# Attention and a squared-ReLU MLP on one core: direct cast loads and PE transposes for the first two batches, v on the software queue, attention ahead of the MLP

## The chip, the cores and the metric

The kernel runs on one core of one Trainium2 chip. The metric is the device time of one execution in microseconds (us). Engines are named as in the profile: PE does matmuls, DVE is VectorE, ACT is ScalarE, POOL is GpSimd, SP is SyncE, which here only issues DMA transfers. "Lnnn" is a line of the kernel. "DMA share" is the mean share of time that the 16 DMA engines of the core spent on packets; it passes 1 when packets overlap. "Clock" is the clock that the throttle granted to PE, as a fraction of full speed.

## The reference

```python
B, H, S, Nb, D = 8, 8, 576, 16, 64          # q, k, v: [B, H, S, D] float32
k_all = concatenate([beacon_k, k], axis=2)   # 16 beacon tokens in front
v_all = concatenate([beacon_v, v], axis=2)
scores = q @ k_all.T / sqrt(D)               # causal mask, beacons always visible
a = softmax(scores)
x = (a @ v_all)  -> [B*S, H*D] = [4608, 512]
h = x @ w_in                                 # w_in  [512, 2048] float32
out = (maximum(h, 0) ** 2) @ w_out           # w_out [2048, 512] float32
```

Attention is done per batch in four pairs of heads. For a pair it is a chain of links: QK (q times k, on PE), the exponential (ACT), the causal mask (DVE), AV (the result times v, on PE), the division by the sum (DVE, which writes x). The MLP is done in nine chunks of 512 tokens; a batch has 576 tokens, so chunk 0 needs batch 0, chunk 1 needs batch 1, and in general chunk j needs batch j (chunk 8 the last batch, 7). Matmuls are in bf16, so q, k, v and both weights must be cast; q and k must also be transposed (the head dimension has to lie on the partitions), and so must x.

## The kernel before

A small list scheduler written in Python decides, at build time, the order of instructions on every engine. An engine then runs its list in order, so an instruction whose data is late stops everything behind it on that engine. A gate holds a pair of heads back until the list has placed so many chunks of MLP work. The path of q and k of each batch is: load by SP into a float32 staging buffer (eight of them), cast by a compute engine, transpose by DMA.

```python
def add_load(b, x, c, prio):                 # 128 tokens of all heads: runs of 64 floats
    ...
    nc.sync.dma_start(out=st[lo:rows], in_=t[b, :, t0:t0 + rows - lo, :].transpose([1, 0, 2]))
    ...
    engs = ("DVE", "ACT", "POOL") if b == 0 else ("POOL",)
    cast[b, x, c] = add(..., engs, ..., emit_cast, deps=deps, give=ld)

def add_trans(b, x, prio):
    ...
            nc.sync.dma_start(               # DMA transpose, on the SP queue
                out=dst[b % 2][:, lo:hi, :, :].rearrange("p c h t -> p (c h) t"),
                in_=srcb[b % 2][:, lo:hi, :].rearrange("p c d -> p (c d)"),
                transpose=True)
...
def gate(o):                                 # when pair p may enter PE's list
    if p < HP: return True
    jj, i = divmod(p - HP, HP)
    return o.progress >= mlp_chunk_us * (jj + (0.0, 0.2, 0.4, 0.6)[i])
...
def add_xt(b):                               # x of a batch: five DMA transposes on the SP queue
    ...
    nc.sync.dma_start(out=xT[:, :, at:at + n], in_=xn[b % 2][0:n, t, :], transpose=True)
```

The weights are cast by their own transfers on the software queue of POOL, once the last load of batch 0 is there. (Cuts are marked with three dots.)

The softmax here doesn't subtract the row's maximum and nothing guards it: scores larger than these inputs give would overflow.

## Time and profile before

The median of three runs was 431.69 us (429.19 to 433.43); with a fourth it was 432.28 us.

| stretch, us | PE busy, us | clock | what happens |
|---|---|---|---|
| 0 to 72 | 14.6 | 0.77 | attention of batch 0, then PE waits for x |
| 72 to 130 | 49.6 | 0.82 | MLP chunk 0, then attention of batch 1 |
| 130 to 300 | 155.7 | 0.94 | steady state, with holes |
| 300 to 429 | nearly all | 0.99 | chunks 6 to 8, pure PE |

The view counts time without a clock record as 1.00. The packed trace's first clock record lies at 35.7 us here, so the clocks shown for the first stretches are too high by an amount that the records don't give.

The page's view of 40 equal slices (10.7 us each), the kernel before; digits are tenths:

```profile
PE   0174003998679995899799979997999999999995
...
PEclk9998555999858998699999989998999999999999
DMA  9799999996979998999899877056002201400202
```

PE is empty in the slices from 43 to 64 us while the DMA engines are full. The busy times of three stretches, the kernel before (after the stretch: its length, then busy us and instructions of PE, PEld, DVE, ACT, POOL, then clock, DMA share, GB/s):

```profile
0.00:72.00 72.00, 14.61 (x169) 8.76 (x170) 12.97 (x38) 17.94 (x24) 18.86 (x35) 0.77 1.08 180
72.00:130.00 58.00, 49.61 (x389) 25.02 (x388) 16.94 (x32) 31.04 (x36) 16.77 (x26) 0.82 0.93 182
130.00:300.00 170.00, 155.68 (x1214) 81.15 (x1213) 54.98 (x96) 84.81 (x96) 43.67 (x68) 0.94 0.89 170
```

The two longest waits of PE, the kernel before (total us, times, longest us):

```profile
PE ps_98 L476 <- DMA xT<-xn_85: 34.7, 1, 34.7
PE ps_95 L344 <- DMA qT_77<-qb_71: 19.7, 2, 15.6
```

PE starts 15.6 us late, because q must be loaded, cast and transposed, and it stands still for 34.7 us ahead of the first MLP matmul, because x must be transposed by DMA. The timeline of the SP queue and of PE, the kernel before, shows the end of that wait (start us, us, what, number):

```profile
52.07 11.26 SPq L431 DMA_TRANSPOSE xT<-xn_85  x5
63.43 8.16 SPq L294 DMA_TRANSPOSE qT_78<-qb_72  x1
...
71.65 3.57 PE L476 MATMUL ps_98<-xT,w_in 128*128 128x512 bf16 x8 [34.74 <-DMA xT<-xn_85]
```

x of batch 0 was complete at 38.4 us, but its transposes stand in SP's list behind the loads of batch 1, are issued only at 52 us, and then take 20 us among the weights. Chunk 1 starts at 128.0 us. The packets, the kernel before:

```profile
DMA packets 185422, 58.10 MB, mean 135 GB/s; under 512 B 176688, under 2 KB 180784, under 8 KB 185392
```

### The profile page before, as it was taken

The numbers are of one execution on the slowest core, as the hardware profiler recorded it, in microseconds if no ns is written. First come the engines' busy times: TensorE is split into PE (matmuls) and PEld (weight loads), VectorE is DVE, ScalarE is ACT, GpSimd is POOL, SyncE is SP. The second block draws the span as 40 slices with busy tenths as digits, with TensorE's granted clock in tenths as the row PEclk, the third lists the DMA queues.
The fourth block names the chain that finished last, engine by engine and source line by source line (L and its number), as shares of the span: only waits on it lengthen the run. The fifth ranks groups of instructions, "written<-read, shape, count | busy, mean of one in ns | idle before, by whom it ended". The sixth has DMA issues, their size and how long they took to land.

```text
span 429.2 us, 6367 instructions
## 1 busy us (share of the span) xinstructions
PE 343.5 (80%) x2560; PEld 171.7 (40%) x2560; DVE 124.4 (29%) x230; ACT 191.1 (45%) x219; POOL 79.3 (18%) x128
## 2 busy tenths in 40 slices
PE   0174003998679995899799979997999999999995
PEld 0033001443444443444444438644454445444442
DVE  1135000311433512252135224512541463130310
ACT  4470000518574447254555455635644664341621
POOL 3034330360123450243222410020000000000000
PEclk9998555999858998699999989998999999999999
DMA  9799999996979998999899877056002201400202
GB/s 168 156 188 197 203 176 195 209 172 151 212 139 189 229 199 187 198 211 188 185 189 199 179 159 147 2 131 146 1 2 73 81 2 50 106 2 0 98 2 98
DMA packets 185422, 58.10 MB, mean 135 GB/s; under 512 B 176688, under 2 KB 180784, under 8 KB 185392
## 3 DMA queue, kind: packets, MB, share of 16 engines
q1 hardware_dynamic: 181168, 53.50, 63.5%
q0 software_dynamic: 4224, 4.19, 6.0%
q8 instruction: 20, 0.33, 0.3%
q14 instruction: 10, 0.08, 0.1%
HBM read 37.22 MB, written 9.44 MB: 109 GB/s over the span
## 4 chain that ended last, share of the span: by engine, by line
PE 62%; SPq 4%; DMA 2%; ACT 2%; DVE 1%; issue 1%; ACTq 0%
PE ps_95 L511 8%; PE ps_96 L476 8%; PE ps_97 L476 7%; PE ps_95 L476 7%; PE ps_97 L511 7%; PE ps_98 L476 6%; PE ps_98 L511 5%; PE ps_96 L511 4%; SPq L294 3%; PE ps_98 L391 3%; SPq L431 1%; DMA xT<-xn_85 1%; PE ps_95 L391 1%; ACT pt_81 L365 1%; PE ps_96 L344 1%; PE ps_96 L391 1%
## 5 line engine op out<-in xcount | busy, mean ns | idle before, releaser
L476 PEld LDWEIGHTS <-w_in 128*128 128x128 bf16 x640 | 63.1, 101 | 109.7 <-issue 55.6
L476 PE MATMUL ps_98<-xT,w_in 128*128 128x512 bf16 (+1 forms) x136 | 33.0, 390 | 34.7 <-DMA xT<-xn_85 34.7
L500 DVE TENSOR_TENSOR g_88<-g_88 128x1024 bf16<-128x1024 bf16 x40 | 28.0, 701 | 93.2 <-ACT g_88 L488 93.2
L476 PE MATMUL ps_96<-xT,w_in 128*128 128x512 bf16 (+1 forms) x176 | 41.2, 384 | 5.4 <-DMA xT<-xn_85 4.5
L511 PEld LDWEIGHTS <-g_88 128*128 128x128 bf16 x320 | 29.8, 98 | 36.4 <-issue 3.1
L476 PE MATMUL ps_97<-xT,w_in 128*128 128x512 bf16 (+1 forms) x168 | 37.1, 367 | 1.9 <-DMA xT<-xn_86 1.9
L511 PEld LDWEIGHTS <-g_89 128*128 128x128 bf16 x256 | 23.7, 98 | 29.0 <-issue 2.8
L476 PE MATMUL ps_95<-xT,w_in 128*128 128x512 bf16 (+1 forms) x160 | 34.6, 361 | 0.0
L500 DVE TENSOR_TENSOR g_89<-g_89 128x1024 bf16<-128x1024 bf16 x32 | 22.3, 697 | 35.9 <-ACT g_89 L488 35.9
L511 PE MATMUL ps_95<-w_out,g_89 128*128 128x512 bf16 x128 | 30.4, 380 | 0.0
L511 PE MATMUL ps_97<-w_out,g_88 128*128 128x512 bf16 x128 | 30.0, 380 | 0.0
L488 ACT ACTIVATE g_88<-ps_98 128x1024 bf16<-128x1024 f32 x8 | 8.2, 1024 | 48.4 <-PE ps_98 L476 48.4
L344 PEld LDWEIGHTS <-kT_79 64*128 64x128 bf16 x192 | 8.7, 106 | 37.8 <-issue 33.1
L511 PE MATMUL ps_96<-w_out,g_88 128*128 128x512 bf16 x96 | 22.7, 379 | 0.0
L511 PE MATMUL ps_98<-w_out,g_89 128*128 128x512 bf16 x96 | 22.7, 379 | 0.0
L344 PE MATMUL ps_95<-qT_77,kT_79 64*128 64x128 bf16 (+3 forms) x38 | 6.0, 371 | 20.6 <-DMA qT_77<-qb_71 19.7
L488 ACT ACTIVATE g_88<-ps_96 128x1024 bf16<-128x1024 f32 x10 | 10.2, 1024 | 15.1 <-PE ps_96 L476 15.1
L374 DVE TENSOR_TENSOR pt_81<-pt_81,tri 128x1024 bf16<-128x1024 bf16 x8 | 5.5, 690 | 38.3 <-ACT pt_81 L365 38.3
L391 PEld LDWEIGHTS <-pt_81 128*128 128x128 bf16 (+1 forms) x240 | 11.9, 120 | 11.3 <-DVE pt_81 L374 8.5
L511 PE MATMUL ps_98<-w_out,g_88 128*128 128x512 bf16 x64 | 15.1, 379 | 0.0
L344 PEld LDWEIGHTS <-kT_80 64*128 64x128 bf16 x192 | 7.6, 96 | 16.4 <-issue 14.2
L374 DVE TENSOR_TENSOR pt_84<-pt_84,tri 128x1024 bf16<-128x1024 bf16 x8 | 6.6, 819 | 26.0 <-ACT pt_84 L365 26.0
(169 smaller groups left out, 466.1 us busy)
## 6 DMA issues: line engine op xcount, KB each, us to landing
out_dram<-osb_90 SPq DMA_DIRECT2D x9, 512.0 KB, 3.3
out_dram<-osb_91 SPq DMA_DIRECT2D x8, 512.0 KB, 3.5
w_in<-in_moe_w_in_dram POOLq DMA_DIRECT2D x4, 512.0 KB, 11.7
w_out<-in_moe_w_out_dram POOLq DMA_DIRECT2D x4, 512.0 KB, 12.8
stg_67<-in_k_dram SPq DMA_DIRECT2D x6, 256.0 KB, 4.2
stg_68<-in_k_dram SPq DMA_DIRECT2D x5, 256.0 KB, 4.2
stg_65<-in_q_dram SPq DMA_DIRECT2D x4, 256.0 KB, 4.8
stg_66<-in_q_dram SPq DMA_DIRECT2D x4, 256.0 KB, 4.3
```

The source lines that it names most:

```text
L294: nc.sync.dma_start(out=dst[b % 2][:, lo:hi, :, :].rearrange("p c h t -> p (c h) t"), in_=srcb[b % 2][:, lo:hi, :].rearrange("p c d -> p ( ...
L344: nc.tensor.matmul(st[:, hj, at:at + 128 * (t1 - t0)], kT[b % 2][hp, c, pr, :], qT[b % 2][hp, t0:t1, pr, :], start=True, stop=True,)
L365: nc.scalar.activation(pt[take_pt.held[2]][:, :, off:off + width], st[:, :, 0:width], AF.Exp, bias=0.0, scale=scale)
L374: nc.vector.tensor_tensor(out=d, in0=d, in1=tri[:, None].to_broadcast([128, 2, 4, 128]), op=ALU.min)
L391: nc.tensor.matmul(a[:, hj, t * (D + 1):(t + 1) * (D + 1)], P[0:rr, hj, o:o + 128], vb[b % 2][0:rr, c, h, :], start=(c == 0), stop=(c == t),)
L431: nc.sync.dma_start(out=xT[:, :, at:at + n], in_=xn[b % 2][0:n, t, :], transpose=True)
L476: nc.tensor.matmul(h[:, u, lo - spans[0][0]:hi - spans[0][0]], w_in_sb[:, mc, ft * 128:(ft + 1) * 128], xT[:, mc, lo % RING:lo % RING + hi ...
L488: nc.scalar.activation(dst, h, AF.Relu, bias=0.0, scale=1.0)
L500: nc.vector.tensor_tensor(out=d, in0=d, in1=d, op=ALU.mult)
L511: nc.tensor.matmul(o[:, ts, :], G[:, fc, (2 * u + ts) * 128:(2 * u + ts + 1) * 128], w_out_sb[:, fc, :], start=(fc == 0), stop=(fc == NFT ...
```

## The change

Its intent is to get PE going early. In batches 0 and 1, q and k come straight from DRAM in bf16, through the casting software queue, one pair of heads at a time, in runs of 1.5 KB (each partition takes six neighbouring tokens); PE transposes them, and also x of these batches. v of batches 1 to 7 moves from the SP queue to the software queue. The gates put attention 0.4 chunk ahead of the MLP. Smaller parts: QK computes 576 queries instead of 640, two buffers instead of one may hold attention output, the table of the exponential is loaded at the start, casts of batch 0 avoid ACT. The weights also start earlier: they wait for the fourth load of v instead of the last load of batch 0, and the traces show w_in issued at 10.3 us instead of 30.5. The diff, cut to its core:

```diff
+    NPE = 2          # batches with direct loads and PE transposes of q, k
+    NXPE = 2         # batches whose x is transposed by PE
...
+        soft = x == "v" and b >= 1
+        queue = nc.gpsimd if soft else nc.sync
...
+    def add_strided(b, prio):
...
+                    nc.gpsimd.dma_start(out=dst[b % 2][:, h],
+                                        in_=t[b, h].rearrange("h (p s) d -> p h s d", s=NS))
...
+                            nc.tensor.transpose(pp[64 * hj:64 * hj + 64, half, at + u * NP:at + (u + 1) * NP],
+                                                t[b % 2][:, 2 * pr + hj, u, :], ident[0:NP, 0:NP])
...
-            return o.progress >= mlp_chunk_us * (jj + (0.0, 0.2, 0.4, 0.6)[i])
+            return o.progress >= mlp_chunk_us * (jj + (-0.4, -0.15, 0.1, 0.35)[i])
...
+    def add_xt_pe(b):
...
+                    nc.tensor.transpose(pp[:, 0, t_start(t):t_start(t) + n],
+                                        xn[b % 2][0:n, t, 128 * pr:128 * pr + 128], ident[0:n, 0:n])
...
-            w_ops["in", i] = add(f"win{i}", "POOL", 1.3, emit, prio=-100 + i, deps=[load0[-1]], dma=3.2)
+            w_ops["in", i] = add(f"win{i}", "POOL", 1.3, emit, prio=-100 + i, deps=[load0[3]], dma=3.2)
```

More of the change, by code (lines that the diff above doesn't have):

```diff
@@ L7 @@
 from concourse._compat import with_exitstack
+from concourse.masks import make_identity
 FP32 = mybir.dt.float32
@@ L19 @@
     __slots__ = ("name", "engs", "dur", "emit", "prio", "need", "users", "left", "ready",
-                 "take", "give", "gate", "held", "dma", "tag", "pe_time")
+                 "take", "give", "gate", "held", "dma", "pe_time", "behind", "followers")
     def __init__(self, name, engs, dur, emit, prio=0.0, deps=(), take=None, give=None,
-                 gate=None, dma=0.0, pe_time=0.0):
+                 gate=None, dma=0.0, pe_time=0.0, behind=()):
         self.name = name
@@ L36, in __init__ @@
         self.pe_time = pe_time
+        self.behind = list(behind)
+        self.followers = []
 class Order:
-    LAT = {"PE": 0.2, "ACT": 0.2, "DVE": 0.15, "POOL": 0.25, "SP": 0.1}
+    LAT = {"PE": 0.2, "ACT": 0.2, "DVE": 0.15, "POOL": 0.25, "SP": 0.1, "-": 0.0}
     def __init__(self, pools, limits):
@@ L58, in run @@
     def run(self):
-        engines = ["PE", "ACT", "DVE", "POOL", "SP"]
+        engines = ["PE", "ACT", "DVE", "POOL", "SP", "-"]
         for op in self.ops:
-            op.left = len(op.need)
+            op.left = len(op.need) + len(op.behind)
             for d in op.need:
                 d.users.append(op)
+            for d in op.behind:
+                d.followers.append(op)
         avail = {e: [] for e in engines}
@@ L102, in run @@
                     for op in avail[e]:
-                        if id(op) in started:
+                        if any(free[x] <= now + 1e-9 for x in op.engs[:op.engs.index(e)]):
                             continue
@@ L122, in run @@
                     started.add(id(op))
+                    for u in op.followers:
+                        u.left -= 1
+                        if u.left == 0:
+                            release(u)
                     for ee in op.engs:
@@ L130, in run @@
                     dur = op.dur[e] if isinstance(op.dur, dict) else op.dur
+                    if e == "SP":
+                        dur = max(dur, dma_free - now - 4.0)
                     end = now + dur
@@ L149, in run @@
         for op, e, _ in issued:
-            op.emit(e)
+            if e != "-":
+                op.emit(e)
         self.issued = issued
@@ L193 @@
     stg = [sb(f"stg{i}", [128, H, D], FP32) for i in range(NSTG)]
-    qb = [sb(f"qb{i}", [128, NT, H * D], BF16) for i in range(2)]
-    kb = [sb(f"kb{i}", [128, NT, H * D], BF16) for i in range(2)]
+    NP = 96
+    NS = S // NP
+    W = HP * NT * 128
+    WS = H * NS * D
+    qk_area = sb("qk_area", [128, 4 * WS], BF16)
+    qb = [qk_area[:, (2 * i) * W:(2 * i + 1) * W].rearrange("p (g c d) -> p g c d", g=HP, c=NT)
+          for i in range(2)]
+    kb = [qk_area[:, (2 * i + 1) * W:(2 * i + 2) * W].rearrange("p (g c d) -> p g c d", g=HP, c=NT)
+          for i in range(2)]
+    qs = [qk_area[0:NP, (2 * i) * WS:(2 * i + 1) * WS].rearrange("p (h s d) -> p h s d", h=H, s=NS)
+          for i in range(2)]
+    ks = [qk_area[0:NP, (2 * i + 1) * WS:(2 * i + 2) * WS].rearrange("p (h s d) -> p h s d", h=H, s=NS)
+          for i in range(2)]
+    bks = [sb(f"bks{i}", [Nb, H, D], BF16) for i in range(2)]
     vb = [sb(f"vb{i}", [128, NT, H, D + 1], BF16) for i in range(2)]
-    qT = [sb(f"qT{i}", [128, NT, HP, 128], BF16) for i in range(2)]
-    kT = [sb(f"kT{i}", [128, NT, HP, 128], BF16) for i in range(2)]
+    qT = [sb(f"qT{i}", [128, HP, NT * 128], BF16) for i in range(2)]
+    kT = [sb(f"kT{i}", [128, HP, NT * 128], BF16) for i in range(2)]
     pt = [sb(f"pt{i}", [128, 2, 2048], BF16) for i in range(NPT)]
     xn = [sb(f"xn{i}", [128, NT, H * D], BF16) for i in range(2)]
+    ident = sb("ident", [128, 128], BF16)
+    warm = sb("warm", [128, 8], FP32)
     xT = sb("xT", [128, NMC, RING], BF16)
@@ L209 @@
         pools={"ps": range(4), "stg": range(NSTG), "pt": range(NPT)},
-        limits={"strip": 2, "av": 1, "mlp": 2},
+        limits={"strip": 2, "av": 2, "mlp": 2, "tp": 1},
     )
     add = order.add
+    nc.vector.memset(warm, 0.0)
+    nc.scalar.activation(warm, warm, AF.Exp)
     for i in range(2):
-        nc.gpsimd.memset(qb[i][:, NT - 1, :], 0.0)
-        nc.gpsimd.memset(kb[i][:, NT - 1, :], 0.0)
-    for i in range(2):
-        nc.vector.memset(qb[i][:, 0, :], 0.0)
-    nc.gpsimd.memset(tri, BIG)
-    for i in range(4):
-        nc.gpsimd.affine_select(out=tri[:, i, :], in_=tri[:, i, :], compare_op=ALU.is_ge, fill=0.0,
-                                base=Nb if i == 0 else 0, pattern=[[1, 128]], channel_multiplier=-1)
+        nc.vector.memset(kT[i][:, :, Nb + S:NT * 128], 0.0)
+        nc.vector.memset(vb[i][:, :, :, D:D + 1], 1.0)
     for p in pt:
@@ L225, with emit_tri @@
             nc.vector.memset(p[:, :, lo:hi], 0.0)
-    for i in range(2):
-        nc.vector.memset(vb[i][:, :, :, D:D + 1], 1.0)
+    nc.vector.memset(tri, BIG)
+    def emit_tri(e):
+        for i in range(4):
+            nc.gpsimd.affine_select(out=tri[:, i, :], in_=tri[:, i, :], compare_op=ALU.is_ge, fill=0.0,
+                                    base=Nb if i == 0 else 0, pattern=[[1, 128]], channel_multiplier=-1)
+    ident_op = add("ident", "POOL", 0.6, lambda e: make_identity(nc, ident), prio=-199.8)
+    tri_op = add("tri", "POOL", 1.0, emit_tri, prio=-150.0)
     def rows_of(c):
@@ L246, with t_rows, t_start, add_zero @@
     load0 = []
-    def q_rows(c):
-        return 128 - Nb if c == 0 else rows_of(c)
+    load_chain = []
+    def t_rows(t):
+        return 128 - Nb if t == 0 else rows_of(t)
+    def t_start(t):
+        return max(0, 128 * t - Nb)
+    NPE = 2
+    NXPE = 2
+    zero_ops = {}
+    strided = {}
+    def add_zero(b):
+        def emit(e):
+            nc.gpsimd.memset(qb[b % 2][:, :, NT - 1, :], 0.0)
+            nc.gpsimd.memset(kb[b % 2][:, :, NT - 1, :], 0.0)
+        deps = trans[NPE - 1, "q"] + trans[NPE - 1, "k"] + trans[NPE - 2, "q"] + trans[NPE - 2, "k"]
+        zero_ops[b] = add(f"zero{b}", "POOL", 1.0, emit, prio=10.0 * b - 1, deps=deps)
     def add_load(b, x, c, prio):
-        rows = q_rows(c) if x == "q" else rows_of(c)
         t, beacon = src[x]
-        box = {}
+        lo = Nb if (c == 0 and beacon is not None) else 0
+        if x == "q":
+            t0, rows = 128 * c, min(128, S - 128 * c)
+        else:
+            t0, rows = t_start(c), rows_of(c)
         def emit_load(e):
             st = stg[ld.held[2]]
-            lo = 0
-            if c == 0 and beacon is not None:
-                lo = Nb
-                nc.sync.dma_start(out=st[0:Nb], in_=beacon[b].transpose([1, 0, 2]))
-            t0 = max(0, 128 * c - Nb)
-            nc.sync.dma_start(out=st[lo:rows], in_=t[b, :, t0:t0 + rows - lo, :].transpose([1, 0, 2]))
-        ld = add(f"ld{b}{x}{c}", "SP", 1.3 if (c == 0 and beacon is not None) else 0.65, emit_load,
-                 prio=prio, take=("stg", "stg"), dma=1.15 * rows / 128)
+            if lo:
+                queue.dma_start(out=st[0:Nb], in_=beacon[b].transpose([1, 0, 2]))
+            queue.dma_start(out=st[lo:rows], in_=t[b, :, t0:t0 + rows - lo, :].transpose([1, 0, 2]))
+        soft = x == "v" and b >= 1
+        queue = nc.gpsimd if soft else nc.sync
+        ld = add(f"ld{b}{x}{c}", "POOL" if soft else "SP", 1.3 if lo else 0.65, emit_load,
+                 prio=prio, take=("stg", "stg"), dma=1.15 * rows / 128,
+                 behind=[strided[0][1, "q"]] if b == 0 else load_chain[-1:] + [strided[min(b, NPE - 1)][HP - 1, "q"]], deps=[w_ops["out", 2]] if b == 1 else ())
+        load_chain.append(ld)
         if b == 0:
@@ L274, in emit_cast @@
             else:
-                dst = (qb if x == "q" else kb)[b % 2][0:rows, c, :]
-                copy_on(e, dst, st[0:rows].rearrange("p h d -> p (h d)"))
+                dst = (qb if x == "q" else kb)[b % 2][0:rows, :, c, :]
+                copy_on(e, dst, st[0:rows].rearrange("p (g u) d -> p g (u d)", u=2))
         deps = [ld]
-        if b >= 2:
-            if x == "v":
-                deps += [av_ops[p] for p in range(HP * (b - 2), HP * (b - 1))]
+        if x == "v" and b >= 2:
+            deps += [av_ops[p] for p in range(HP * (b - 2), HP * (b - 1))]
+        if x != "v":
+            if b < NPE + 2:
+                deps += [zero_ops[b]]
             else:
                 deps += trans[b - 2, x]
-        engs = ("DVE", "ACT", "POOL") if b == 0 else ("POOL",)
-        cast[b, x, c] = add(f"cast{b}{x}{c}", engs, {"DVE": 0.65, "ACT": 0.65, "POOL": 1.1}, emit_cast,
+        engs = ("POOL", "DVE") if b == 0 else ("POOL",)
+        cast[b, x, c] = add(f"cast{b}{x}{c}", engs, {"DVE": 0.6, "POOL": 0.65}, emit_cast,
                             prio=prio, deps=deps, give=ld)
@@ L289, in add_trans @@
         srcb, dst = (qb, qT) if x == "q" else (kb, kT)
-        groups = [(c, c + 1) for c in range(NT)] if b == 0 else [(0, NT)]
-        ops = []
-        for lo, hi in groups:
-            def emit(e, lo=lo, hi=hi):
-                nc.sync.dma_start(
-                    out=dst[b % 2][:, lo:hi, :, :].rearrange("p c h t -> p (c h) t"),
-                    in_=srcb[b % 2][:, lo:hi, :].rearrange("p c d -> p (c d)"),
-                    transpose=True,
-                )
-            deps = [cast[b, x, c] for c in range(lo, hi)]
-            if b >= 2:
-                deps += [qk_ops[p, i] for p in range(HP * (b - 2), HP * (b - 1)) for i in range(4)]
-            ops.append(add(f"tr{b}{x}{lo}", "SP", 0.4 + 0.64 * (hi - lo), emit, prio=prio, deps=deps,
-                           dma=0.64 * (hi - lo)))
@@ L304, in add_trans, with emit @@
-        trans[b, x] = ops
+        def emit(e):
+            nc.sync.dma_start(
+                out=dst[b % 2].rearrange("p g (c t) -> p (g c) t", c=NT),
+                in_=srcb[b % 2].rearrange("p g c d -> p (g c d)"),
+                transpose=True,
+            )
+        deps = [cast[b, x, c] for c in range(NT)]
+        deps += [qk_ops[p, i] for p in range(HP * (b - 2), HP * (b - 1)) for i in range(4)]
+        trans[b, x] = [add(f"tr{b}{x}", "SP", 3.8, emit, prio=prio, deps=deps, dma=3.2)]
@@ new lines, in add_strided, with emit_bk, emit, emit_tp @@
+    def add_strided(b, prio):
+        loads = {}
+        def emit_bk(e):
+            nc.gpsimd.dma_start(out=bks[b % 2], in_=beacon_k[b].transpose([1, 0, 2]))
+        after = [w_ops["out", 3]] if b == 1 else [strided[b - 1][HP - 1, "q"]] if b else []
+        free = trans[b - 2, "q"] + trans[b - 2, "k"] if b >= 2 else []
+        bk = None
+        trans[b, "q"], trans[b, "k"] = [], []
+        for pr in range(HP):
+            h = slice(2 * pr, 2 * pr + 2)
+            for n, (x, t, dst) in enumerate((("k", k, ks), ("q", q, qs))):
+                def emit(e, t=t, dst=dst, h=h):
+                    nc.gpsimd.dma_start(out=dst[b % 2][:, h],
+                                        in_=t[b, h].rearrange("h (p s) d -> p h s d", s=NS))
+                loads[pr, x] = add(f"sld{b}{x}{pr}", "POOL", 0.7, emit, prio=prio + pr + 0.1 * n, behind=after, deps=free,
+                                   dma=0.95)
+            if pr == 0:
+                bk = add(f"sldbk{b}", "POOL", 0.7, emit_bk, prio=prio + 0.05, behind=after, deps=free, dma=0.1)
+        strided[b] = loads
+        for pr in range(HP):
+            h = slice(2 * pr, 2 * pr + 2)
+            box = {}
+            def emit_tp(e, pr=pr, h=h, box=box):
+                pp = ps[box["t"].held[2]].bitcast(BF16)
+                nc.tensor.transpose(pp[:, 1, 0:Nb], bks[b % 2][:, h, :], ident[0:Nb, 0:Nb])
+                for half, at, t in ((1, Nb, ks), (0, 0, qs)):
+                    for u in range(NS):
+                        for hj in range(2):
+                            nc.tensor.transpose(pp[64 * hj:64 * hj + 64, half, at + u * NP:at + (u + 1) * NP],
+                                                t[b % 2][:, 2 * pr + hj, u, :], ident[0:NP, 0:NP])
+            busy = [qk_ops[HP * (b - 2) + pr, i] for i in range(4)] if b >= 2 else []
+            tp = add(f"tp{b}.{pr}", "PE", 1.3, emit_tp, prio=100.0 * (HP * b + pr) - 190,
+                     deps=[bk, loads[pr, "k"], loads[pr, "q"], ident_op] + busy, take=("ps", "tp"))
+            box["t"] = tp
+            def emit_k(e, pr=pr, box=box):
+                pp = ps[box["t"].held[2]].bitcast(BF16)
+                copy_on(e, kT[b % 2][:, pr, 0:Nb], pp[:, 1, 0:Nb])
+                copy_on(e, kT[b % 2][:, pr, Nb:Nb + S].rearrange("p (n s) -> p n s", s=NS),
+                        pp[:, 1, Nb:Nb + S].rearrange("p (s n) -> p n s", s=NS))
+            def emit_q(e, pr=pr, box=box):
+                pp = ps[box["t"].held[2]].bitcast(BF16)
+                copy_on(e, qT[b % 2][:, pr, 0:S].rearrange("p (n s) -> p n s", s=NS),
+                        pp[:, 0, 0:S].rearrange("p (s n) -> p n s", s=NS))
+            ek = add(f"ek{b}.{pr}", "DVE", 0.9, emit_k, prio=-200.0, deps=[tp])
+            eq = add(f"eq{b}.{pr}", ("DVE", "ACT"), 0.75, emit_q, prio=-199.0, deps=[tp])
+            add(f"tpg{b}.{pr}", "-", 0.0, None, prio=0.0, deps=[ek, eq], give=tp)
+            trans[b, "k"].append(ek)
+            trans[b, "q"].append(eq)
@@ L307 @@
     PIECES = [
-        ([(0, 0, 4, 0)], 0, 512),
-        ([(1, 1, 5, 0)], 512, 464),
-        ([(2, 2, 5, 0), (0, 4, 5, 336)], 1024, 416),
-        ([(3, 3, 5, 0), (4, 4, 5, 208)], 1536, 288),
+        ([(0, 0, 496, 0)], 0, 496),
+        ([(1, 112, 576, 0)], 512, 464),
+        ([(2, 240, 576, 0), (0, 496, 576, 336)], 1024, 416),
+        ([(3, 368, 576, 0), (4, 496, 576, 208)], 1536, 288),
     ]
@@ L315, in pt_off @@
         if c == 0:
-            return 128 * t if t < 4 else 1360
+            return t_start(t) if t < 4 else 1360
         if c == 4:
@@ L332, in gate @@
             jj, i = divmod(p - HP, HP)
-            return o.progress >= mlp_chunk_us * (jj + (0.0, 0.2, 0.4, 0.6)[i])
+            return o.progress >= mlp_chunk_us * (jj + (-0.4, -0.15, 0.1, 0.35)[i])
         exps = []
         for i, (mms, off, width) in enumerate(PIECES):
-            cols = sum(128 * (t1 - t0) for _, t0, t1, _ in mms)
+            cols = sum(max(96, t1 - t0) for _, t0, t1, _ in mms)
             def emit_qk(e, i=i, mms=mms):
@@ L344, in emit_qk @@
                         nc.tensor.matmul(
-                            st[:, hj, at:at + 128 * (t1 - t0)],
-                            kT[b % 2][hp, c, pr, :],
-                            qT[b % 2][hp, t0:t1, pr, :],
+                            st[:, hj, at:at + t1 - t0],
+                            kT[b % 2][hp, pr, 128 * c:128 * c + 128],
+                            qT[b % 2][hp, pr, t0:t1],
                             start=True, stop=True,
                         )
-            need_c = {c for c, _, _, _ in mms}
-            need_t = {t for _, t0, t1, _ in mms for t in range(t0, t1)}
-            if b == 0:
-                deps = [trans[b, "k"][c] for c in need_c] + [trans[b, "q"][t] for t in need_t]
+            if b < NPE:
+                deps = [trans[b, "k"][pr], trans[b, "q"][pr]]
             else:
@@ L357, in add_pair @@
             if i == 0:
-                take_pt = add(f"pt{p}", "POOL", 0.0, lambda e: None, prio=base, deps=deps,
+                take_pt = add(f"pt{p}", "-", 0.0, None, prio=base, deps=deps,
                               take=("pt", "pt"), gate=gate)
-            qk_ops[p, i] = add(f"qk{p}.{i}", "PE", 0.12 + cols / 2400.0, emit_qk, prio=base + i,
+            qk_ops[p, i] = add(f"qk{p}.{i}", "PE", 0.05 + cols / 2400.0, emit_qk, prio=base + i,
                                deps=deps + [take_pt], take=("ps", "strip"), gate=gate)
@@ L378, in emit_mask @@
                                     op=ALU.min)
-        mask = add(f"mask{p}", "DVE", 0.85, emit_mask, prio=base, deps=exps)
+        mask = add(f"mask{p}", "DVE", 0.95, emit_mask, prio=base, deps=exps + [tri_op])
         def emit_av(e):
@@ L422, with ring_deps, feeds @@
     s2_first = {}
+    def ring_deps(lo, hi):
+        deps = []
+        for j in range(NCH):
+            if j * TCH < hi - RING and (j + 1) * TCH > lo - RING:
+                deps += [s1_ops[j, f] for f in range(NFT // 2)]
+        return deps
+    def feeds(o, lo, hi):
+        for j in range(NCH):
+            if j * TCH < hi and (j + 1) * TCH > lo:
+                xt_of_chunk[j].append(o)
     def add_xt(b):
         for t in range(NT):
-            n = q_rows(t)
-            tok = b * S + max(0, 128 * t - Nb)
+            n = t_rows(t)
+            tok = b * S + t_start(t)
             def emit(e, n=n, t=t, tok=tok):
@@ L431, in emit, with emit_tp, emit_ev @@
                 nc.sync.dma_start(out=xT[:, :, at:at + n], in_=xn[b % 2][0:n, t, :], transpose=True)
-            deps = [norm_ops[HP * b + i] for i in range(HP)]
-            for j in range(NCH):
-                if j * TCH < tok + n - RING and (j + 1) * TCH > tok - RING:
-                    deps += [s1_ops[j, f] for f in range(NFT // 2)]
-            o = add(f"xt{b}.{t}", "SP", 1.2, emit, prio=-50.0 + b, deps=deps, dma=0.64 * n / 128)
-            xt_ops[b, t] = o
-            for j in range(NCH):
-                if j * TCH < tok + n and (j + 1) * TCH > tok:
-                    xt_of_chunk[j].append(o)
+            deps = [norm_ops[HP * b + i] for i in range(HP)] + ring_deps(tok, tok + n)
+            o = add(f"xt{b}.{t}", "SP", 1.28, emit, prio=-50.0 + b, deps=deps, dma=0.64 * n / 128)
+            xt_ops[b, t] = o
+            feeds(o, tok, tok + n)
+    def add_xt_pe(b):
+        for pr in range(HP):
+            box = {}
+            def emit_tp(e, pr=pr, box=box):
+                pp = ps[box["t"].held[2]].bitcast(BF16)
+                for t in range(NT):
+                    n = t_rows(t)
+                    nc.tensor.transpose(pp[:, 0, t_start(t):t_start(t) + n],
+                                        xn[b % 2][0:n, t, 128 * pr:128 * pr + 128], ident[0:n, 0:n])
+            tp = add(f"xtp{b}.{pr}", "PE", 0.35, emit_tp, prio=-120.0, deps=[norm_ops[HP * b + pr]],
+                     take=("ps", "tp"))
+            box["t"] = tp
+            def emit_ev(e, pr=pr, box=box):
+                pp = ps[box["t"].held[2]].bitcast(BF16)
+                copy_on(e, xT[:, pr, (b * S) % RING:(b * S) % RING + S], pp[:, 0, 0:S])
+            o = add(f"xte{b}.{pr}", ("ACT", "DVE"), {"ACT": 0.67, "DVE": 0.72}, emit_ev, prio=-110.0,
+                    deps=[tp], give=tp)
+            xt_ops[b, pr] = o
+            feeds(o, b * S, b * S + S)
     w_ops = {}
@@ L481, in add_chunk @@
             s1_ops[j, f] = add(f"s1.{j}.{f}", "PE", 1.73, emit_s1, prio=base + f,
-                               deps=xt_of_chunk[j] + [w_ops["in", f // 2]], take=("ps", "mlp"), pe_time=1.73)
+                               deps=xt_of_chunk[j] + [w_ops["in", f // 2]] + [s2_ops[j - 2, u] for u in range(2) if j >= 2], take=("ps", "mlp"), pe_time=1.73)
             def emit_relu(e, f=f):
@@ L500, in emit_sq @@
                 nc.vector.tensor_tensor(out=d, in0=d, in1=d, op=ALU.mult)
-            sq.append(add(f"sq{j}.{f}", "DVE", 0.62, emit_sq, prio=-10.0, deps=[rl]))
+            sq.append(add(f"sq{j}.{f}", "DVE", 0.7, emit_sq, prio=-10.0, deps=[rl]))
         for u in range(2):
@@ L547 @@
     st_ops = {}
-    b0 = [("k", 0), ("q", 0), ("q", 1), ("q", 2), ("q", 3), ("k", 1), ("q", 4), ("k", 2), ("k", 3), ("k", 4)]
+    nat = [("k", 0), ("q", 0), ("q", 1), ("q", 2), ("q", 3), ("k", 1), ("q", 4), ("k", 2), ("k", 3), ("k", 4)]
     for b in range(B):
-        n = 0
         lp = 10.0 * b
-        for x, c in b0 + [("v", c) for c in range(NT)]:
+        if b < NPE:
+            add_strided(b, lp - 200.0 if b == 0 else lp)
+        if NPE <= b < NPE + 2:
+            add_zero(b)
+        for n, (x, c) in enumerate(([] if b < NPE else nat) + [("v", c) for c in range(NT)]):
             add_load(b, x, c, lp + 0.1 * n)
-            n += 1
-        add_trans(b, "k", lp - 5.0)
-        add_trans(b, "q", lp - 5.1)
+        if b >= NPE:
+            add_trans(b, "k", lp - 5.0)
+            add_trans(b, "q", lp - 5.1)
         if b == 0:
@@ L562 @@
             add_pair(b, pr)
-        add_xt(b)
+        if b < NXPE:
+            add_xt_pe(b)
+        else:
+            add_xt(b)
         for j in range(NCH):
```

## The prediction

> **What bounds it now.** By busy time in stretches, PE works 14.3 us of the first 72: it starts at 15.6, stops at 37 and begins the MLP only at 71.6, released by the DMA transpose of xT (34.7 us, PE's longest wait). In that gap the granted clock is 0.50 and the DMA share over 1. The timeline shows why: w_in and w_out land in about 12 us each, and the SP queue is blocked behind its own issues (xT transposes 11.3 us, one qT transpose 8.2). From 72 to 294 us PE is busy 200 of 222 us at DMA share 0.91, with holes at 100-130 and 160-180 where attention waits for exp and mask at clock 0.5-0.8, and chain pieces of 2-4 us of SP queue and xT at 168, 243-256 and 284-294. From 294 to 424 PE is busy 128.5 of 130 us at clock 0.99: pure PE.
>
> **What the change does.** 176,688 of 185,422 packets are under 512 B. The Trainium skill ("DMA: Bandwidth & Descriptors", Specifications) gives 512 B as the least transfer for line rate; the trace agrees in that DMA is full at 150-215 GB/s. For batches 0 and 1, q and k come as 1.5 KB runs, cast underway, first pair first: 16 loads instead of 20 staged loads, 20 casts and 12 transposes (3.2-6 us each to landing). I estimate 20-25 us of DMA time gone. Added: 200 PE transposes and 40 for x, estimated at 60-100 ns from the 65-column matmul intervals, 15-20 us of PE, mostly in former idle time, and 16 evictions of 0.7-0.9 us. QK narrows from 640 to 576 queries, about 3 us. v loads move to POOL, where they issue between casts (0.62 us).
>
> **Sum.** First transposes at 5-7 us; batch 0 attention is then ACT-bound (16 exps, 14 us) to about 24; chunk 0 starts at 27-32 instead of 71.6. w_out lands at about 45, batch 1's loads at 50-55. In PE's order two QK pieces of batch 2 stand before chunk 1, and these need zeroing, staged loads, casts and two 4 us DMA transposes: I expect a new PE hole of 10-20 us in 65-90. So chunk 1 starts at 80-87 instead of 128. From there 8 chunks of 27.7 us and 24 pairs of 2.3 us are 277 us, stalls and cold clock 10-15, the tail 5: about 380 us. DMA, at about 33 us per batch against 37 of PE, does not take the gain back.
>
> **Time: 380 us, range 365 to 402.** Chances: faster by over 2% 0.95, within 2% 0.04, slower 0.01.
>
> **Shown right or wrong by.** Chunk 0's first matmul near 30 us; PE's wait for xT under 5 us; packets under 512 B down by some 30,000; PE busy within 5 us of 346; a wait of QK of batch 2 on qT/kT's DMA at 65-90; after 100 us PE busy over 95%; holes at 100-130 gone, attention being 0.4 chunk ahead.
>
> **What would make it wrong.** Software-queue v loads (1,024 descriptors each) could issue slowly: the skill ("SBUF — State Buffer", SBUF: two separate sides, the box on "DVE blocks DMA") says VectorE's fast modes lock POOL out while it writes descriptors; this trace has POOL casts of 1.02-1.12 us beside 0.62, in line with a lock. Then POOL's in-order queue delays casts too, and later batches run DMA-paced: up to 400. If weights land after 45 us, chunk 0's second half stalls. If the clock stays 0.5 through attention of batches 0 and 1, add 5-8 us. If the hole before chunk 1 doesn't come, 366-370.

## The result and the profile after

The changed kernel took 370.67 us (median of 4 runs, 367.46 to 371.41) against 432.28 us. The ratio is 0.857, with a 95% interval of 0.850 to 0.864. Ratios here are the mean time of one kernel's fast runs over that of the kernel before in the same rounds, so they are not quite the ratio of the medians.

The same slices, the changed kernel (9.2 us each):

```profile
PE   1987999889989999799995999999999999999995
...
PEclk9998999989999999989997899999999999999999
DMA  8999996999999999999995999310131014002003
```

The same stretches, the changed kernel:

```profile
0.00:72.00 72.00, 59.06 (x644) 32.95 (x645) 29.03 (x72) 41.44 (x53) 40.56 (x70) 0.98 1.10 186
72.00:130.00 58.00, 53.97 (x497) 26.82 (x494) 29.94 (x48) 33.90 (x41) 29.26 (x42) 0.97 1.15 196
130.00:300.00 170.00, 163.85 (x1368) 82.98 (x1366) 68.87 (x117) 91.88 (x106) 47.00 (x69) 0.97 0.70 137
```

PE now does 59 us of work in the first 72 us instead of 15, at the same DMA share. In the later stretches it is busier too, and the granted clock is higher (0.97 against 0.82 and 0.94). The three longest waits of PE, the changed kernel:

```profile
PE ps_96 L380 <- DMA bks_72<-in_beacon_k_dram: 7.3, 1, 7.3
PE ps_98 L608 <- DMA xT<-xn_84: 4.2, 1, 4.2
PE ps_97 L608 <- DMA xT<-xn_85: 1.9, 1, 1.9
```

The first is the start of the kernel. The other two lie at 195 and 154 us, at the x of batches that are still transposed by DMA. The start of chunk 0 and of chunk 1 and the first QK of batch 2 in the timeline, the changed kernel (L447 is QK, L608 the first MLP matmul):

```profile
31.90 3.22 PE L608 MATMUL ps_98<-xT,w_in 128*128 128x512 bf16 x8
...
77.50 0.59 PE L447 MATMUL ps_98<-qT_76,kT_78 64*128 64x496 bf16 x2 [0.28 <-DMA kT_78<-qk_area]
...
79.29 1.90 PE L608 MATMUL ps_98<-xT,w_in 128*128 128x512 bf16 x8
```

Chunk 0 starts 40 us earlier, chunk 1 49 us earlier. Its packets:

```profile
DMA packets 123535, 51.93 MB, mean 140 GB/s; under 512 B 109488, under 2 KB 116656, under 8 KB 123504
```

### The profile page after: what moved, and what is told of

It reads as the page before. It is cut to its first block, busy times and chain, and to the rows that moved or that the text cites. A ratio compares the mean times of both kernels' runs of the same rounds, so it can differ in the third digit from the quotient of the medians.

```text
span 369.7 us, 6756 instructions
## 1 busy us (share of the span) xinstructions
PE 342.0 (92%) x2800; PEld 172.0 (47%) x2800; DVE 139.5 (38%) x252; ACT 189.7 (51%) x221; POOL 116.8 (32%) x180
## 2 busy tenths in 40 slices
DMA packets 123535, 51.93 MB, mean 140 GB/s; under 512 B 109488, under 2 KB 116656, under 8 KB 123504
## 4 chain that ended last, share of the span: by engine, by line
PE 77%; DMA 11%; SPq 3%; ACT 3%; DVE 2%; issue 1%; POOL 1%; ACTq 0%; DVEq 0%; POOLq 0%
PE ps_96 L643 10%; PE ps_99 L608 9%; PE ps_98 L643 8%; PE ps_98 L608 8%; PE ps_96 L608 8%; PE ps_97 L643 8%; PE ps_97 L608 7%; PE ps_99 L643 6%; DMA kT_79<-qk_area 3%; PE ps_96 L492 2%; DMA stg_66<-in_q_dram 2%; PE ps_97 L492 2%; PE ps_97 L447 2%; DMA qk_area<-in_q_dram 2%; DMA stg_63<-in_k_dram 2%; SPq L544 1%
## 5 line engine op out<-in xcount | busy, mean ns | idle before, releaser
L608 PEld LDWEIGHTS <-w_in 128*128 128x128 bf16 x640 | 60.8, 99 | 70.0 <-issue 10.1
L632 DVE TENSOR_TENSOR g_89<-g_89 128x1024 bf16<-128x1024 bf16 x40 | 28.6, 717 | 55.9 <-ACT g_89 L620 55.9
L608 PE MATMUL ps_98<-xT,w_in 128*128 128x512 bf16 (+1 forms) x152 | 36.9, 391 | 4.2 <-DMA xT<-xn_84 4.2
L608 PE MATMUL ps_99<-xT,w_in 128*128 128x512 bf16 (+1 forms) x200 | 39.9, 345 | 0.0
L632 DVE TENSOR_TENSOR g_90<-g_90 128x1024 bf16<-128x1024 bf16 x32 | 22.5, 702 | 38.6 <-ACT g_90 L620 38.6
L608 PE MATMUL ps_97<-xT,w_in 128*128 128x512 bf16 (+1 forms) x152 | 31.0, 351 | 1.9 <-DMA xT<-xn_85 1.9
L608 PE MATMUL ps_96<-xT,w_in 128*128 128x512 bf16 x136 | 32.2, 379 | 0.0
L643 PE MATMUL ps_96<-w_out,g_90 128*128 128x512 bf16 x96 | 24.5, 401 | 0.0
L643 PE MATMUL ps_98<-w_out,g_89 128*128 128x512 bf16 x96 | 23.8, 393 | 0.0
L643 PE MATMUL ps_96<-w_out,g_89 128*128 128x512 bf16 x96 | 22.7, 379 | 0.3 <-ACT qT_77 L265 0.3
L475 DVE TENSOR_TENSOR pt_80<-pt_80,tri 128x1024 bf16<-128x1024 bf16 x8 | 6.0, 747 | 35.7 <-ACT pt_80 L466 34.3
L265 ACT COPY osb_91<-ps_96 128x1024 f32<-128x1024 f32 x3 | 3.0, 1012 | 23.8 <-PE ps_96 L643 12.0
L643 PE MATMUL ps_97<-w_out,g_90 128*128 128x512 bf16 x64 | 15.2, 380 | 0.0
L643 PE MATMUL ps_99<-w_out,g_89 128*128 128x512 bf16 x64 | 15.2, 380 | 0.0
L643 PE MATMUL ps_98<-w_out,g_90 128*128 128x512 bf16 x64 | 15.2, 380 | 0.0
L643 PE MATMUL ps_97<-w_out,g_89 128*128 128x512 bf16 x64 | 15.1, 379 | 0.0
L620 ACT ACTIVATE g_89<-ps_98 128x1024 bf16<-128x1024 f32 x8 | 8.2, 1023 | 12.6 <-PE ps_98 L608 12.6
L620 ACT ACTIVATE g_89<-ps_96 128x1024 bf16<-128x1024 f32 x9 | 9.2, 1023 | 8.2 <-PE ps_96 L608 8.1
L466 ACT ACTIVATE pt_80<-ps_99 128x992 bf16<-128x992 f32 (+3 forms) x9 | 7.9, 879 | 9.5 <-PE ps_99 L447 9.0
## 6 DMA issues: line engine op xcount, KB each, us to landing
w_in<-in_moe_w_in_dram POOLq DMA_DIRECT2D x4, 512.0 KB, 12.2
```

The lines of the kernel that those rows point to most:

```text
L265: nc.scalar.copy(dst, src)
L466: nc.scalar.activation(pt[take_pt.held[2]][:, :, off:off + width], st[:, :, 0:width], AF.Exp, bias=0.0, scale=scale)
L475: nc.vector.tensor_tensor(out=d, in0=d, in1=tri[:, None].to_broadcast([128, 2, 4, 128]), op=ALU.min)
L608: nc.tensor.matmul(h[:, u, lo - spans[0][0]:hi - spans[0][0]], w_in_sb[:, mc, ft * 128:(ft + 1) * 128], xT[:, mc, lo % RING:lo % RING + hi ...
L620: nc.scalar.activation(dst, h, AF.Relu, bias=0.0, scale=1.0)
L632: nc.vector.tensor_tensor(out=d, in0=d, in1=d, op=ALU.mult)
```

## The experiments

The result holds at least three changes that could each carry the gain. My theory was that the front end does it (direct loads and PE transposes of batches 0 and 1). The rivals were that v off the SP queue does it, by unblocking SP, and that the earlier attention does it. The table gives all runs. "Chunk 1" and "chunk 2" are the starts of the first ReLU of that chunk in the profiled run, 2 to 4 us after its first matmul; where the profiled run fell over 1.5% above the fastest run of the same kernel, they are left out.

| run | median, us | ratio to before, 95% interval | chunk 0 | chunk 1 | chunk 2 |
|---|---|---|---|---|---|
| before | 430.8 to 432.3 | 1 | 75.2 | 131.6 | 176.8 |
| changed | 370.7 | 0.857 (0.850 to 0.864) | 35.2 | 81.2 | 120.0 |
| e1 front end undone | 407.0 | 0.943 (0.938 to 0.949) | - | - | - |
| e2 v on SP | 367.1 | 0.854 (0.849 to 0.858) | 34.0 | 80.9 | 120.1 |
| e3 old gates | 383.4 | 0.890 (0.884 to 0.896) | 34.0 | 81.5 | 130.9 |
| e4 before, new gates | 408.7 | 0.949 (0.944 to 0.954) | 75.2 | 129.7 | 165.6 |
| e5 x by DMA | 379.5 | 0.879 (0.874 to 0.884) | 53.4 | 97.2 | 140.8 |
| e6 q, k staged, x by PE | 407.3 | 0.944 (0.939 to 0.949) | 47.1 | 104.0 | 170.2 |
| e7 batch 0 only | 380.0 | 0.881 (0.876 to 0.885) | 35.2 | 84.8 | 143.0 |
| e8 runs of 256 B | 372.3 | 0.859 (0.853 to 0.866) | 37.3 | 82.9 | 120.7 |
| e9 changed again | 370.1 | 0.857 (0.852 to 0.862) | 34.1 | 81.6 | 120.0 |
| e10 v on SP, gates at -0.6 | 364.8 | 0.847 (0.844 to 0.850) | 34.4 | 81.4 | 122.5 |
| e11 v on SP, x of 0, 1, 3, 4 by PE | 362.7 | 0.841 (0.838 to 0.845) | 32.5 | 79.6 | 119.1 |
| e12 v on SP, front end for 3 batches | 361.7 | 0.840 (0.837 to 0.843) | 33.8 | 81.3 | 121.3 |

All runs gave correct results. Medians are of all runs of a kernel (e1, e8 and e9 had one slow run each). e1 to e4, e5 to e8 and e9 to e12 ran together, each group on one chip with its own runs of the kernel before.

### e1: the front end undone

```diff
-    NPE = 2
-    NXPE = 2
+    NPE = 0          # q, k of all batches: staged, cast, DMA transposes (batch 0 in five pieces, as before)
+    NXPE = 0
...
-            w_ops["in", i] = add(..., deps=[load0[3]], dma=3.2)
+            w_ops["in", i] = add(..., deps=[load0[-1]], dma=3.2)
...
```

> The changed kernel with its front end undone: q and k of batches 0 and 1 are again staged, cast and transposed by DMA, x of all batches is transposed by DMA, the weights wait for the last load of batch 0; v on the software queue, the earlier attention and the rest of the change stay. Theory (the front end carries the gain): chunk 0 starts after 60 us, chunk 1 after 115 us, the time is 410 to 430 us. Rival 1 (moving v off the SP queue carries it) and rival 2 (the earlier attention carries it): below 395 us.

The three fast runs took 404.5, 406.9 and 407.1 us (the fourth, 412.2 us, was slow). This is 36 us above the changed kernel, so the front end carries more than half of the 62 us gained. But it is also 24 us below the kernel before, and just under the 410 us that I had set as the lower end. Something else is worth 24 us. The early start of the weights is undone together with the loads here and in e6 (w_in at 30.3 and 30.1 us), so its own share of the front end was not tested.

### e2: v on the SP queue again

```diff
-        soft = x == "v" and b >= 1
+        soft = False
```

> The changed kernel with v of all batches on the SP queue again, nothing else. Theory: v's queue matters little, chunk 1 is delayed by a few us at most, 370 to 380 us, because the DMA engines carry the same bytes either way. Rival 1 (v off the SP queue carries the gain): SP blocks behind v and the transposes come late, 395 us or more.

It took 367.1 us: beside the front end, the move of v to the software queue gives nothing. Without the front end it gives little at most: e1, which has it, ends 2 us from e4 below, which does not. Rival 1 has fallen. What the move does change is the number of packets. The packet line of e2, to be read beside that of the changed kernel above:

```profile
DMA packets 154447, 51.93 MB, mean 142 GB/s; under 512 B 142640, under 2 KB 149808, under 8 KB 154416
```

With v on SP there are 30,912 packets more, for the same bytes, and no more time.

### e3 and e4: the gates, in the changed kernel and in the one before

```diff
# e3, in the changed kernel
-            return o.progress >= mlp_chunk_us * (jj + (-0.4, -0.15, 0.1, 0.35)[i])
+            return o.progress >= mlp_chunk_us * (jj + (0.0, 0.2, 0.4, 0.6)[i])
# e4, in the kernel before
-            return o.progress >= mlp_chunk_us * (jj + (0.0, 0.2, 0.4, 0.6)[i])
+            return o.progress >= mlp_chunk_us * (jj + (-0.4, -0.15, 0.1, 0.35)[i])
```

> The changed kernel with the attention gates of before (0, 0.2, 0.4, 0.6 of a chunk instead of -0.4 to 0.35). Theory: the holes at 100 to 200 us grow or shrink by a few us, 368 to 382 us. Rival 2 (the earlier attention carries the gain): 390 us or more.

> The kernel before with only the new gates (-0.4, -0.15, 0.1, 0.35). Theory: the first 72 us don't change, and the holes at 100-130 and 160-180 us shrink little since the DMA sets when q and k are there: 422 to 436 us. Rival 2: 410 us or less.

Both answers went beyond my theory. Putting the old gates back costs the changed kernel 13 us (383.4 us, just above the range). Giving the kernel before the new gates, four numbers, takes 22 us off it (408.7 us, far under the 422 that I had expected, and inside the 410 or less that I had reserved for rival 2). The stretches of e4:

```profile
0.00:72.00 72.00, 15.45 (x169) 9.52 (x171) 13.20 (x38) 18.05 (x24) 18.66 (x35) 0.79 1.07 180
72.00:130.00 58.00, 47.45 (x390) 23.82 (x393) 17.02 (x32) 31.29 (x37) 16.92 (x26) 0.91 0.99 182
130.00:300.00 170.00, 163.36 (x1378) 84.02 (x1398) 80.57 (x126) 89.84 (x104) 45.79 (x68) 1.00 0.90 171
```

The first 130 us are nearly as before, as I had expected. The gain is after that: PE busy 163.4 us of 170 instead of 155.7, and at clock 1.00 instead of 0.94. The starts of the chunks say the same: the lead of e4 over the kernel before is 1.9 us at chunk 1, 11.2 at chunk 2, 17.9 at chunk 5 and 22.2 at chunk 8. In the kernel before, the attention that a chunk needs sits at the end of the chunk before it, with little else to run between its links (QK, exp, mask, AV, normalise, transpose). PE waits at those links, and the waits cost twice, because the clock falls: the kernel before has 0.83 and 0.66 in the stretches from 160 to 170 and 170 to 180 us. The stretch from the first ReLU of chunk 1 to that of chunk 8 gives the sizes (the kernel before, then e4, then the changed kernel):

```profile
131.60:398.60 267.00, 251.76 (x1881) 125.82 (x1880) 88.91 (x152) 131.83 (x148) 43.37 (x67) 0.96 0.61 122
129.70:376.40 246.70, 239.63 (x1853) 119.46 (x1880) 102.32 (x161) 122.21 (x139) 46.02 (x68) 1.00 0.67 134
81.20:339.20 258.00, 250.15 (x1961) 123.53 (x1962) 101.20 (x164) 132.95 (x151) 71.73 (x105) 0.98 0.71 134
```

The first two load the same 1,880 weights (28 matmuls of e4 have no record). Of the 20 us that e4 saves, about 8 are idle time (15.2 to 7.1 us) and about 12 are the same matmuls taking less time at the higher clock. The Trainium skill ("TensorE: Matmul & The Clock Gate", Part 1: The HAM clock gate) says that the full clock is granted on recent activity, and that an idle window of about 3.4 us takes it back to half speed. The records show 0.50 through the idle stretch from 40 to 70 us, and the first eight matmuls of chunk 0 in the kernel before come 0.43 us apart, later ones 0.216 us (1.73 us for eight). With attention 0.4 chunk ahead, there are MLP matmuls to lay between those links: after chunk 1, the waits of PE for the mask come to 4.9 us in the kernel before, and e4 shows none.

Front end and gates together make a table of two by two, medians in us. (The row without the front end is the kernel before, so the smaller parts of the change are in the other row.)

| | old gates | new gates |
|---|---|---|
| without front end | 430.8 | 408.7 |
| with front end | 383.4 | 370.1 to 370.7 |

The front end is worth 47 us with the old gates and 38 with the new ones, the gates 22 without and 13 with it. About 9 us can be had from either. Without the front end, the smaller parts together are worth little: e1, which has most of them (not the casts off ACT) and the new gates but no front end, is 2 us from e4. With the front end, the gates act early: e3 starts chunk 1 with the changed kernel (81.5 and 81.2 us), but chunk 2 comes 11 us later, most of its 13. The last division of batch 2 comes at 109.9 us instead of 102.9, its transposes of x are issued at 116.7 instead of 109.3, and PE waits for them (e3):

```profile
127.32 0.58 PE L608 MATMUL ps<-xT,w_in 128*128 128x512 bf16 x1 [6.49 <-DMA xT<-xn]
```

### e5, e6 and e7: what in the front end

```diff
# e5, in the changed kernel
-    NXPE = 2
+    NXPE = 0
# e6, in e1
-    NXPE = 0
+    NXPE = 2
# e7, in the changed kernel
-    NPE = 2
+    NPE = 1
...
```

> The changed kernel with x of batches 0 and 1 transposed by DMA again (q and k keep their direct loads and PE transposes). If the xT transposes behind the weights were a large part of the front end's gain: a PE wait on xT of over 10 us before chunk 0 and again before chunk 1, 385 to 398 us. If the loads of q and k carry it alone: under 378 us.

> The front end undone as in the first run, but x of batches 0 and 1 stays on PE. If direct loads of q and k carry most of the front end: 398 to 406 us, close to the 407 of all undone. If the x transposes carry most: under 388 us. With the run before this makes a two by two table; unequal differences say that the parts need each other.

> The changed kernel with the direct loads and PE transposes of q and k for batch 0 only; batch 1 is staged and transposed by DMA. Theory: chunk 0 starts at 32 us as in the changed kernel, chunk 1 starts 5 to 20 us later than 79 us, 375 to 392 us. If only the very start matters: within 4 us of 370.

Transposing x on PE is worth 9 us when q and k come directly (379.5 against 370.7 us), and nothing when they are staged (407.3 against 407.0 us). e6 is the run to look at: its chunk 0 starts 28 us earlier than that of the kernel before, its chunk 1 also 28 us earlier, and it still ends with e4 and e1. Its stretches:

```profile
0.00:72.00 72.00, 33.94 (x270) 16.69 (x273) 18.49 (x44) 24.72 (x30) 31.92 (x55) 0.95 1.05 183
72.00:130.00 58.00, 46.41 (x403) 23.22 (x407) 21.50 (x36) 31.02 (x39) 26.47 (x40) 0.91 1.24 188
130.00:300.00 170.00, 154.15 (x1314) 79.53 (x1330) 61.97 (x104) 96.26 (x109) 58.73 (x87) 0.96 0.85 161
```

The first 72 us gain 19 us of PE work on the kernel before, and as much on e4. The lead is lost between chunk 1 and chunk 2, the stretch of e6 and, after it, that of e4:

```profile
104.00:170.20 66.20, 47.52 (x428) 22.88 (x434) 25.42 (x41) 32.45 (x40) 28.00 (x43) 0.88 1.19 181
129.70:165.50 35.80, 34.96 (x265) 16.34 (x267) 14.79 (x24) 19.15 (x22) 14.29 (x21) 1.00 1.04 186
```

There e6 is idle for 18.7 us, and it still has more of the attention of batch 2 to do. The SP queue and PE of e6, from its timeline, show the new waits:

```profile
86.77 9.66 SPq L355 DMA_TRANSPOSE qT<-qk_area  x1
97.57 9.82 SPq L355 DMA_TRANSPOSE kT<-qk_area  x1
...
109.51 0.58 PE L460 MATMUL ps<-qT,kT 64*128 64x496 bf16 x4 [3.79 <-DMA kT<-qk_area]
...
166.55 0.58 PE L621 MATMUL ps<-xT,w_in 128*128 128x512 bf16 x1 [5.96 <-DMA xT<-xn]
```

The staged batches follow each other on the DMA at their own pace (q of batch 1, 2 and 3 enters its transpose at 58, 87 and 119 us), and chunk 2 starts at 170.2 us, 5 us behind e4. An earlier chunk 0 moved the wait to batch 2, no more (and PE also waited 6.8 us for w_out, which starts late in e6). In the changed kernel, q of batch 2 enters its transpose at 63.4 us, so its chunk 2 starts at 120 us.

e7 says the same about batch 1: chunk 1 is only 4 us later than in the changed kernel, but chunk 2 is 23 us later, and the whole takes 9 us more. Of the expectations, that for e7's time held (375 to 392 us), but its delay showed at chunk 2, not at chunk 1, where I had put 5 to 20 us. e5 fell between its two alternatives (under 378, or 385 and more): x on PE is a real part, but the smaller one. e6 came out at the upper end of "direct loads carry most", just above it.

### e8: the length of the runs

```diff
-                                        in_=t[b, h].rearrange("h (p s) d -> p h s d", s=NS))
+                                        in_=t[b, h].rearrange("h (s p) d -> p h s d", s=NS))
...
-                copy_on(e, qT[b % 2][:, pr, 0:S].rearrange("p (n s) -> p n s", s=NS),
-                        pp[:, 0, 0:S].rearrange("p (s n) -> p n s", s=NS))
+                copy_on(e, qT[b % 2][:, pr, 0:S], pp[:, 0, 0:S])
```

(The eviction of k likewise.) The same 16 loads on the same queue, in runs of 256 B.

> The changed kernel with the same 16 direct loads in runs of 256 B instead of 1.5 KB (token order changes, evictions are plain copies). If the run length is what makes the loads cheap: the loads of batch 0 land later by 3 us or more, weights and batch 1 follow, 374 to 384 us. If what counts is that staging, casts and DMA transposes are gone: within 3 us of 370.

The packet line of e8:

```profile
DMA packets 138895, 51.93 MB, mean 142 GB/s; under 512 B 127920, under 2 KB 132016, under 8 KB 138864
```

There are 15,360 packets more than in the changed kernel, which is 16 loads of 192 runs cut in six. Chunk 0 starts 2 us later, chunk 2 0.7 us later, and the time, 372.3 us, is within the noise of the changed kernel's. So the 1.5 KB runs are not what makes the front end fast. What is left of it, by elimination, is that the staging, the casts and the DMA transposes of two batches are gone from a full DMA and from the SP queue, and that the weights start earlier. No run takes these apart.

### e9 to e12: a better version

e9 is the changed kernel unedited. The others start from e2 and add one thing each:

```diff
# e10
-            return o.progress >= mlp_chunk_us * (jj + (-0.4, -0.15, 0.1, 0.35)[i])
+            return o.progress >= mlp_chunk_us * (jj + (-0.6, -0.35, -0.1, 0.15)[i])
# e11
-        if b < NXPE:
+        if b in (0, 1, 3, 4):
# e12
-    NPE = 2
-    NXPE = 2
+    NPE = 3
+    NXPE = 3
```

> The changed kernel again, on the same chip and in the same rounds as the three after it: 368 to 373 us. It says whether the 367 us with v on the SP queue is a real gain of one per cent over the changed kernel.

> v on the SP queue and the gates moved earlier by another 0.2 chunk (-0.6 to 0.15). If attention further ahead keeps paying, the two waits of 3.9 and 1.7 us on the DMA transpose of x (at 155 and 198 us) go and it takes 361 to 366 us. If q and k from the DMA set the pace there, the wait moves to qT or kT and it takes 366 to 371 us.

> v on the SP queue, and x of batches 3 and 4 transposed on PE as well as of 0 and 1. The two waits of 3.9 and 1.7 us on xT go, and 40 more PE transposes cost about 4 us: 363 to 368 us, near even. If the DMA relieved of these transposes helps the loads after them, towards 363.

> v on the SP queue, and the direct loads and PE transposes for three batches instead of two. It adds 6 to 7 us of PE work in a stretch where PE is already 95% busy and removes DMA traffic that is hidden there: 370 to 378 us, slower. If the DMA still paced the kernel at 100 to 200 us: 362 us or less.

The changed kernel repeated to 370.1 us. e11 (362.7 us) and e12 (361.7 us) beat both kernels in the same rounds; their intervals lie below that of e9, and e12 over e9 is 0.840 / 0.857 = 0.981. e2, their starting point, ran in other rounds on another chip; its interval (0.849 to 0.858) lies above both of theirs too. e12 was a miss: I had expected it to be slower, for 6 to 7 us of added transposes. The longest waits of PE in e12:

```profile
PE ps L380 <- DMA bks<-in_beacon_k_dram: 7.2, 1, 7.2
PE ps L559 <- DVE xn L507: 4.3, 5, 1.2
PE ps L492 <- DVE pt L475: 1.1, 2, 0.6
```

No wait on xT or kT is left, where e2 still had 5.6 us on xT, and PE's busy time is 339.1 us, 2.9 us below that of the changed kernel though it has 120 more matmuls, for its clock is 0.993 instead of 0.976. So the DMA had still held PE up after 100 us. But e11, which takes only the x of two more batches off the DMA, is as fast within the intervals, so what the third batch of q and k adds is not shown. e10 gained less (364.8 us), with 3.0 us on xT left, and its interval touches that of e2, so a gain of still earlier gates is not shown. e9 and e10 came out as expected, e11 0.3 us below its range. Whether v on SP by itself is better than on the software queue is not settled: the intervals of e2 and e9 overlap.

## Why the prediction was right, and where it was not

The time, 380 us predicted and 370.7 measured, and the class were right. The number alone says little of the reasons: with the old gates (e3, 383.4 us) it would have fitted better still, so the hit does not bear out what the prediction says of the gates. Point by point:

- **Chunk 0 near 30 us, chunk 1 at 80 to 87.** Measured 31.9 and 79.3 us, so this step held. First transposes at 5 to 7: 7.3 us, just late. Batch 0's attention took longer than said: its last AV began at 29.2 us, not 24, partly because PE ran cold (24 transposes took 1.17 to 1.32 us there, and 0.70 us once warm).
- **A new hole of 10 to 20 us in 65 to 90, for q and k of batch 2.** Wrong. In 70 to 80 us PE was idle for 2.7 us, and the wait on kT was 0.28 us. The forecast had batch 2 ready at about 80 to 87 and PE free at about 65 to 70. PE in fact reached that QK at 77 us, since MLP and attention of batch 1 lay interleaved until then, and the transposes, issued at 63.4 and 67.1 us, landed just as PE came. The mechanism was there, and its two times fell together instead of apart. The prediction had set 366 to 370 us for a kernel without this hole, and 370.7 was measured. It explains at most some 4 us of the miss, though: chunk 1 came 4 us before the middle of its range (79.3 against 83.5 us), and the stretch after it, forecast at about 296 us, took 290 (369.7 less 79.3).
- **PE total of 346, within 5 us.** 342.0 us. The PE transposes cost 13.4 us (7.8 + 1.4 + 4.1), not 15 to 20.
- **After 100 us, PE busy over 95%.** 257.3 of 269.7 us, 95.4%.
- **PE's wait for xT under 5 us.** Missed: 6.1 us, all of it later, at batches that still use the DMA.
- **Holes at 100 to 130 gone, "attention being 0.4 chunk ahead".** They are gone (PE busy 28.3 of 30 us), and it took both parts. The gates alone do not do it: e4 is busy 19.8 of 30 us there and, like the kernel before (7.2 us), waits for masks (7.7 us). The front end alone (e3) ends the waits for masks but is busy only 21.1 of 30 us; instead it has the 6.5 us wait for x shown above. So "attention being 0.4 chunk ahead" was half of the reason.
- **The gain put down to chunk 1's start.** This step was mis-sized: the prediction gave no size to the gates, which are worth 22 us alone and 13 with the front end. "DMA does not take the gain back" held. With the old gates, the front end brings chunk 1 forward by 50 us (131.6 to 81.5) and chunk 8 by 48 (398.6 to 350.7). With the new gates it is 48 and 37 (e4 to the changed kernel, 129.7 to 81.2 and 376.4 to 339.2), but those 11 us are not waiting: between these two points PE is idle for 7.8 us in the changed kernel and 7.1 in e4 (the lines from chunk 1 to chunk 8 under e4). They are busy time, 250.2 against 239.6 us. I estimate 3 to 4 us of it as attention of batch 2 that e4 had done before its chunk 1 (16 QK and 60 AV matmuls, at 0.085 and 0.033 us each in the traces); the clock, 0.98 against 1.00, may account for much of the rest. The 7.8 us of idle time (1.7, 1.9 and 4.2 us near 105, 155 and 197 us, all on DMA transposes) are what the DMA still costs, and what e11 and e12 go after.
- **Packets under 512 B down by some 30,000, and the skill's least size of 512 B.** They fell by 67,200. From the kernel before to e2 the fall is 34,048, close to the forecast; the other 33,152 come with v's move to the software queue, which it forgot, and are v's 256-byte runs (7 batches of 592 tokens and 8 heads). The number of small packets is not shown to cost time: e8 adds 15,360 back and e2 33,152, at no cost outside noise. So packet size was not a reason that the runs bear out, though the forecast of DMA relief was right.
- **The danger of slow issue on POOL.** It did not show. Each v load was issued in 0.74 to 0.92 us and landed in 3.7 to 12.2 us.

## What to carry to other kernels

When an early stage of an in-order pipeline is made faster, look for the next stage's inputs before counting the gain: e6 brought chunk 1 forward by 28 us and ended where it would have ended without. Where attention or any chain with short links feeds dense matmuls, start it before its consumer has run dry; here four numbers in a gate were worth 22 us in the old kernel, because they keep PE's clock up as well as its list full. And test a reason by itself even if the forecast came true: packet size, a reason of the prediction, and v's queue, a part of the change, turned out to carry nothing that the runs can show.

## What the Trainium skill lacked or had wrong

- "DMA: Bandwidth & Descriptors", Specifications, gives 512 B as the least transfer for line rate. Here, with the DMA share over 1 in any case, the same loads in runs of 256 B and of 1.5 KB gave 372.3 and 370.7 us. The page does not say that the loss need not reach the time: the 256 B runs cost about 2 us at chunk 0, 0.7 at chunk 2 and nothing outside noise at the end.
- The same page does not say that, on the hardware queue, a trace counts every 256-byte run as a packet of its own: the same v loads give 30,912 fewer packets on the software queue (123,535 against 154,447 in all), where the trace shows them as 1,904 packets of 4,096 B and 336 of 2,048 B.
- "SBUF — State Buffer", SBUF: two separate sides, warns that VectorE can starve descriptor writing on POOL. No run here shows a cost: 35 loads of v on POOL, beside a VectorE that is 38% busy, against the SP queue made 370.7 against 367.1 us, with overlapping intervals.
- "TensorE: Matmul & The Clock Gate", Part 4: PE-mode transpose, says that the full clock does not engage for transposes and measures about 275 ns for one of 128x128 in a kernel. Here one of 128x128 took 217 to 222 ns amid warm matmuls and 313 before PE was warm, and 24 of 96x64 in a row took 0.70 us and 1.17 to 1.32 us. So transposes gain when PE is already warm; whether they can warm it by themselves, no run shows.
- The same page, in Part 1, warns that clock records are not fully to be trusted; it lacks this case. The traces have no clock record at all before 35.7 us (the kernel before) and 24.4 us (the changed kernel), which the view shows as 1.00. Pairs of QK matmuls of 512 columns start 0.43 us apart at 16 us in the kernel before; pairs of 496 columns in the changed kernel start 0.37 us apart at 11 us and 0.21 at 70.6 us. So PE ran at about half its later pace at these points, where the view shows 1.00.
